# First MoE's first layer on scaled fp16 pairs, its weights converted two chunks at a time

## The chip, the cores and the metric

One core of one Trainium2 chip runs the kernel. The metric is the device time of one execution in microseconds (us), the median of several runs; lower is better. Beside it one execution was recorded by the hardware profiler; all rows of a trace come from such an execution.

## The reference

Causal attention with a cumulative bias over 4 batches of 8 heads, 576 tokens of 64 dimensions, then two pairs of layers (MoE blocks) over the 2304 tokens:

```python
cum = np.cumsum(np.maximum(s, 0.0), axis=-1)
bias = -(cum[:, :, :, None] - cum[:, :, None, :])
scores = np.where(causal, -1e9, q @ k.T / 8 + np.minimum(bias, 0.0))
attn = softmax(scores)                       # rows; then attn @ v
x = heads_to_columns(attn @ v)               # (2304, 512), float32
h = x @ moe_w_in                             # (512, 2048)
x = (h * np.tanh(np.log1p(np.exp(h)))) @ moe_w_out
h = x @ moe2_w_in
out = (h / (1.0 + np.exp(-1.702 * h))) @ moe2_w_out
```

The weights come as float64, everything else as float32.

## The kernel before

Precision is kept by splitting each factor of a product in a high and a low part and summing three products (`mm3`, L814: high x high, high x low, low x high). In attention's scores and in the first MoE both parts are fp32r tiles; in the second MoE both are fp16, after a scaling by a power of two.

**First MoE's first layer.** Tokens are taken in nine units of 256 (`U`), the 2048 hidden columns in 16 chunks of 128 (`NF`). For a unit and a chunk `l1_mm` (L819) issues 4 x 3 matmuls of 128x256. `first_layer` (L968) does units 0 to 6 (192 matmuls each, group "h<-xh,w" in the trace) while attention still runs: after each chunk `slot_a` lets a share of attention's steps (`tick`, L680) pass. The last two units are done together after attention (L1071, group "acc<-xh,w"), then the products with w_out ("acc<-gh,w"). The results go to HBM (`h_d`) by way of "hs" tiles.

**The weights of that layer.** A chunk arrives as 512 KB of float64 words (`fetch_w`, L742; tile "wst"). It is turned to float32 in three instructions (ScalarE Prelu on the high words, VectorE shift of the low words, VectorE join), then split: ScalarE copies the high part, POOL subtracts to get the low part (`turn_w` L764; in the ordered start `turn_words`, `turn_join`, `turn_parts`, L792 to L812). Chunks 0 to 4 are converted in the ordered start, the others by `bg_a` (L835), three chunks ahead of their use. Twelve chunks are fetched at once (`UP`). Raw chunks and converted ones share pool `wa_p` of 16 buffers of 4 KB; "hs" and the maxima's loads "vl" come from `mo_a` (`MA` = 5).

**x.** When a tile of 128 tokens is done, `emit_tile` (L619) transposes it on TensorE ("xt"), ScalarE copies the high part to the unit's tile ("xh"), VectorE subtracts for the low one.

**Order.** From L852 to L937 `nc.mode = "strict"` ties every instruction to the one before it on its engine, so in this start (the first six of attention's steps, chunks 0 to 4, x of unit 0) each engine keeps the order of the code; `warm(n)` there issues n matmuls that compute nothing. Behind it a planner orders the work by its own costs and readiness; what an engine then executes is a fixed in-order list. Attention's steps of batches 1 to 3 send the probabilities through a DMA transpose ("pt<-hl"); their use waits `LAG` steps. PSUM has 8 banks: 4 for attention's tiles ("s", `ps_s`), 3 for "h", 1 for "o".

## Time and profile before

| | us |
|---|---|
| median of 3 runs | 1001.59 (1001.03 to 1003.63) |
| the profiled execution | 1001.29 |
| its span, first to last instruction | 999.3 |
| TensorE busy | 968.8 (97%) |
| VectorE busy | 676.8 (68%) |
| ScalarE busy | 554.3 (55%) |
| POOL busy | 289.1 (29%) |

PE is TensorE's matmuls, PEld its weight loads, which overlap them; DVE is VectorE, ACT ScalarE, POOL GpSimd. Ends of matmuls are modelled, so the mean of one is a latency: for the rate one reads how many of them start in a stretch. The profile attributes almost all instructions to L79, a helper that records them, so groups are told apart by the names of their tiles.

### The profile page before, as it was taken

Reading aid. Unit: us, or ns where it says so; the run is one execution under the profiler, and the core shown is the slowest. Engines: PE = TensorE matmul, PEld = TensorE weight load, DVE = VectorE, ACT = ScalarE, POOL = GpSimd, SP = SyncE. Lnnn points to the kernel's source line nnn. Section 1 sums busy time; section 2 is a strip of 40 time slices with the busy share of each in tenths; the row PEclk is TensorE's granted clock in tenths of the full one; section 3 lists DMA queues with packets and bytes.
Section 4 is the critical chain, followed back from the end, with each engine's and each line's share of the span. In section 5 each row is a group of like instructions: output and inputs, shape, how many; then the busy total and the mean of one; then the engine's idle time right before and its main releaser. Section 6 shows DMA issues by size and latency. Waiting matters only on the chain.

```text
span 999.3 us, 20234 instructions
## 1 busy us (share of the span) xinstructions
PE 968.8 (97%) x7974; PEld 863.0 (86%) x7974; DVE 676.8 (68%) x1363; ACT 554.3 (55%) x1062; POOL 289.1 (29%) x358
## 2 busy tenths in 40 slices
PE   8989998989999999999999999999999999999997
PEld 6868996979889889998888888888888888888886
DVE  6878677774666874788997967985554654653553
ACT  5656577785667874786565845643333433333331
POOL 5636442442144330000000000054342424333341
PEclk9999999999999999999999999999999999999999
DMA  9931688996689977899995653400100100000000
GB/s 257 342 88 40 186 192 166 178 239 149 157 167 223 191 144 188 308 330 357 380 308 181 233 187 107 127 1 16 49 22 1 44 23 1 22 22 1 22 13 32
DMA packets 157262, 142.26 MB, mean 142 GB/s; under 512 B 90000, under 2 KB 126352, under 8 KB 157168
## 3 DMA queue, kind: packets, MB, share of 16 engines
q1 hardware_dynamic: 150240, 122.22, 43.9%
q0 software_dynamic: 6928, 18.75, 6.9%
q8 instruction: 63, 1.03, 0.4%
q14 instruction: 31, 0.25, 0.1%
HBM read 89.09 MB, written 32.58 MB: 122 GB/s over the span
## 4 chain that ended last, share of the span: by engine, by line
PE 83%; DMA 5%; DVE 4%; issue 2%; ACT 1%; POOL 0%; SPq 0%; DVEq 0%; POOLq 0%; ACTq 0%
PE h L79 31%; PE acc L79 25%; PE p L79 16%; PE s L79 5%; PE o L79 3%; DMA pt<-hl 3%; PE kt L79 1%; PE qt L79 1%; DMA qraw<-in_q_dram 1%; PE pt L79 1%; DMA vraw<-in_v_dram 1%; DVE w2l L79 1%; PE xt L79 0%; DVE P L79 0%; DMA vl<-in_v_dram 0%
## 5 line engine op out<-in xcount | busy, mean ns | idle before, releaser
L79 PE MATMUL h<-x,w2i 128*128 128x256 f16 x1728 | 199.8, 273 | 0.9 <-DVE z L79 0.9
L79 PE MATMUL h<-xh,w 128*128 128x256 f32 x1344 | 189.7, 290 | 1.7 <-POOL w L79 0.9
L79 PEld LDWEIGHTS <-w2i 128*128 128x128 f16 x1728 | 169.0, 98 | 20.7 <-issue 1.1
L79 PE MATMUL acc<-gh,w 128*128 128x512 f32 (+1 forms) x640 | 181.7, 369 | 0.0
L79 PEld LDWEIGHTS h<-xh,w 128*128 128x128 f32 x1344 | 169.1, 192 | 4.1 <-ACT w L79 1.5
L79 PE MATMUL p<-w2h,gl 128*128 128x256 f16 x504 | 136.1, 273 | 0.5 <-DVE gl L79 0.5
L79 PE MATMUL p<-w2l,gh 128*128 128x256 f16 x504 | 136.1, 273 | 0.0
L79 PEld LDWEIGHTS acc<-gh,w 128*128 128x128 f32 x640 | 116.1, 189 | 20.6
L79 PE MATMUL p<-w2h,gh 128*128 128x256 f16 x504 | 133.5, 273 | 0.2 <-DVE e L79 0.2
L79 PE MATMUL acc<-gl,w 128*128 128x512 f32 (+1 forms) x320 | 117.9, 368 | 0.0
L79 POOL TENSOR_TENSOR s<-z 128x256 f32<-128x256 f32 x72 | 54.8, 783 | 216.9 <-DVE z L79 213.3
L79 DVE TENSOR_TENSOR gl<-z,gh 128x1024 fp32r<-128x1024 f32 (+1 forms) x72 | 94.4, 1313 | 26.8 <-ACT gh L79 26.1
L79 ACT ACTIVATE sg<-h,spx 128x512 f32<-128x512 f32 x72 | 49.0, 680 | 110.5 <-PE h L79 110.5
L79 PEld LDWEIGHTS <-gh 128*128 128x128 f16 x1008 | 98.6, 98 | 11.7 <-issue 0.3
L79 DVE SCALAR_TENSOR_TENSOR z<-h,sg 128x512 f32<-128x512 f32 x72 | 49.5, 687 | 72.3 <-ACT sg L79 72.3
L79 ACT ACTIVATE P<-P,mx 128x384 f32<-128x384 f32 (+4 forms) x128 | 76.5, 599 | 34.8 <-DVE mx L79 33.1
L79 DVE TENSOR_TENSOR gl<-s,gh 128x1024 f16<-128x1024 f32 x36 | 44.3, 1232 | 64.3 <-ACT gh L79 64.3
L79 DVE CUSTOM_DVE_ANT_0 P<-s,ck 128x384 f32<-128x384 f32 (+4 forms) x128 | 61.6, 497 | 34.2 <-PE s L79 26.8
L79 ACT ACTIVATE gh<-z 128x1024 fp32r<-128x1024 f32 (+1 forms) x72 | 67.9, 947 | 28.5 <-DVE z L79 25.4
L79 ACT ACTIVATE gh<-s 128x1024 f16<-128x1024 f32 x36 | 38.0, 1057 | 81.3 <-POOL s L79 81.3
L79 PE MATMUL s<-kw,qw 128*128 128x288 f32 (+4 forms) x352 | 78.5, 333 | 3.1 <-DVE mx L79 1.8
L79 DVE SCALAR_TENSOR_TENSOR wst<-wst 128x512 int32<-128x512 int32 x96 | 70.9, 755 | 2.8 <-ACT wst L79 2.5
(146 smaller groups left out, 1635.1 us busy)
## 6 DMA issues: line engine op xcount, KB each, us to landing
h_d<-hs SPq DMA_DIRECT2D x36, 512.0 KB, 4.6
hg<-h_d SPq DMA_DIRECT2D x36, 512.0 KB, 6.2
wst<-in_moe_w_in_dram SPq DMA_DIRECT2D x32, 512.0 KB, 7.2
wst<-in_moe_w_out_dram SPq DMA_DIRECT2D x32, 512.0 KB, 6.1
x_d<-x SPq DMA_DIRECT2D x18, 256.0 KB, 3.4
out_dram<-o SPq DMA_DIRECT2D x9, 512.0 KB, 2.8
kraw<-in_k_dram POOLq DMA_DIRECT2D x32, 128.0 KB, 4.7
w_d<-w2y SPq DMA_DIRECT2D x16, 256.0 KB, 5.1
```

Source lines behind the costliest of these rows:

```text
L79: r = f(*a, **kw)
```

## The change

The first layer of the first MoE goes from fp32r parts to fp16 parts of scaled numbers. The weights are scaled per pair of chunks by a power of two, from a sum of absolute values: ScalarE sums each row (Abs with an accumulator), a bf16 matrix of ones on TensorE sums over the rows (`over_rows`), VectorE makes the scale. x of batches 1 to 3 keeps the scale that v had (now a power of two, no longer divided out in `norm_tile`), x of batch 0 is scaled per unit by v's maxima (`v_peak`, `x_scale`). The eviction from PSUM multiplies by the inverse scales (`evict`), in two pieces where a unit crosses a batch. Chunks are converted in pairs, by two queues of stages (`pair_a`, `pair_b`, `pairs_to`); the low part of a pair's first chunk is made by VectorE, that of its second by POOL in two instructions. A pair of chunks takes one 4 KB buffer instead of two; "hs" and "vl" tiles move to that pool. Sizes and lags change (`MA`, `MBB`, `HLB`, `PTB`, `LAG`).

```diff
-MA = 5
-MBB = 2
+MA = 2
+MBB = 5
-HLB = 3
+HLB = 4
-PTB = 5
-WAH = 3
-NP0 = 5
-FROM = 7
+PTB = 7
-LAG = 4
+LAG = 5
...
+    def to_scale(t, src, tiny, top):
+        nc.vector.tensor_scalar(out=t, in0=src, scalar1=tiny, scalar2=1.0 / top, op0=ALU.max, op1=ALU.mult)
+        nc.vector.reciprocal(t, t)
+        pow2(t)
+
+    def over_rows(cols, n):
+        ps = ps_s.tile([128, 512], F32, tag="s", name="bd")
+        nc.tensor.matmul(out=ps[:, 0:n], lhsT=ones, rhs=cols, start=True, stop=True, skip_group_check=True)
+        return ps[:, 0:n]
...
+    def v_peak(i, g):
+        n = min(128, S - 128 * i)
+        peak(vm0[:n, 2 * i + g:2 * i + g + 1], vt[0, i, g][:n].rearrange("p h d -> p (h d)"))
+
+    def x_scale(k, ni):
+        t = sm_p.tile([128, 2], F32, tag="sx", name="sx", bufs=3)
+        ps = over_rows(vm0[:, 0:2 * ni], 2 * ni)
+        nc.vector.tensor_reduce(out=t[:, 0:1], in_=ps, axis=mybir.AxisListType.X, op=ALU.max)
+        to_scale(t[:, 0:1], t[:, 0:1], 1.0e-30, VTOP)
+        ev_table(k, t)
...
-            t = tmp_pair(F32, "vl")[:, 0:VW]
+            t = wa_p.tile([128, 1024], F32, tag="w", name="vl")[:, 0:VW]
...
-                xunit[u] = xh_a.tile([128, 2, KC, U], F32R, tag="xh", name="xh")
+                xunit[u] = xh_a.tile([128, 2, KC, U], F16, tag="xh", name="xh")
...
+            if b:
+                nc.scalar.activation(out=hi, in_=src, func=AF.Copy)
+                nc.vector.tensor_tensor(out=lo, in0=src, in1=hi, op=ALU.subtract)
+            else:
+                k_ = f"u{u}"
+                k_ = sx[k_][:, 0:1]
+                nc.scalar.activation(out=hi, in_=src, func=AF.Copy, scale=k_)
+                nc.vector.scalar_tensor_tensor(out=lo, in0=src, scalar=k_, in1=hi, op0=ALU.mult, op1=ALU.subtract)
...
+    def pair_sum(p):
+        wsm[p] = ws = sm_p.tile([128, 2], F32, tag="wsm", name="wsm")
+        for e in range(2):
...
+            lut(junk, y, AF.Abs, accum_out=ws[:, e:e + 1])
+
+    def pair_a(p):
+        pair_words(p)
+        pair_join(p)
+        pair_sum(p)
+
+    def pair_col(p):
+        wmx[p] = t = sm_p.tile([128, 2], BF16, tag="wmx", name="wmx")
+        nc.vector.tensor_copy(t, wsm.pop(p))
+
+    def pair_scale(p):
+        ps = over_rows(wmx.pop(p), 2)
+        wkp[p] = k = sm_p.tile([128, 2], F32, tag="wk", name="wk")
+        k = k[:, 0:1]
+        nc.vector.tensor_reduce(out=k, in_=ps, axis=mybir.AxisListType.X, op=ALU.max)
+        to_scale(k, k, TINY, WTOP1)
+        nc.vector.reciprocal(isw[:, p:p + 1], k)
+
+    def pair_parts(p):
+        k = wkp.pop(p)[:, 0:1]
+        win_t[p] = t = wa_p.tile([128, 2, 2, DM], F16, tag="w", name="w")
+        for e in range(2):
+            y = fetched.pop((0, 2 * p + e, "in"))
+            hi, lo = t[:, e, 0, :], t[:, e, 1, :]
+            nc.scalar.activation(out=hi, in_=y, func=AF.Copy, scale=k)
+            if e:
+                nc.gpsimd.tensor_scalar(out=y, in0=y, scalar1=k, scalar2=None, op0=ALU.mult)
+                nc.gpsimd.tensor_tensor(out=lo, in0=y, in1=hi, op=ALU.subtract)
+            else:
+                nc.vector.scalar_tensor_tensor(out=lo, in0=y, scalar=k, in1=hi, op0=ALU.mult, op1=ALU.subtract)
+        fetch_a()
...
+    def pairs_to(pa, pb):
+        for k, f, n in ((0, pair_a, pa), (1, pair_b, pb)):
+            while wq[k] < min(n, NF // 2):
...
```

The ordered start: the steps of the chunks leave it, those of pairs 0 and 1 come in:

```diff
     early_pt(steps[0])
     warm(12)
-    turn_words(0)
+    pair_words(0)
+    for g in range(2):
+        v_peak(0, g)
     score(2)
     early_turn(1, 1)
+    early_pt(steps[1])
+    pair_join(0)
+    early_av(steps[0])
+    score(3)
     load_group(0, 2, 0, False)
...
-    early_pt(steps[1])
-    turn_join(0)
-    early_av(steps[0])
-    turn_parts(0)
-    turn_words(1)
-    score(3)
     early_pt(steps[2])
     early_av(steps[1])
-    turn_join(1)
-    turn_parts(1)
-    emit_tile(steps[1])
-    turn_words(2)
+    pair_sum(0)
+    for g in range(2):
+        v_peak(1, g)
+    emit_tile_turn(steps[1])
+    x_scale("u0", 2)
+    emit_tile_parts(steps[1])
     score(4)
+    pair_col(0)
     early_pt(steps[3])
     early_av(steps[2])
-    turn_join(2)
+    pair_scale(0)
+    pair_words(1)
     score(5)
-    turn_parts(2)
-    turn_words(3)
+    pair_parts(0)
+    pair_join(1)
     early_pt(steps[4])
     early_av(steps[3])
     warm(10)
-    turn_join(3)
+    pair_sum(1)
     early_pt(steps[5])
-    turn_parts(3)
-    turn_words(4)
     warm(4)
+    pair_col(1)
     early_av(steps[4])
+    pair_scale(1)
     early_av(steps[5])
-    turn_join(4)
-    emit_tile(steps[5])
-    turn_parts(4)
+    emit_tile_turn(steps[5])
     warm(8)
+    emit_tile_parts(steps[5])
+    pair_parts(1)
...
     def first_layer(u, xr, each):
         for m in range(0, NF, 4):
-            t = tmp_pair(F32, "hs")
+            t = wa_p.tile([128, 1024], F32, tag="w", name="hs")
...
-                    while wq and (0, min(NF - 1, m + 2 * e + d + WAH)) not in win_t:
-                        bg_a()
+                    p = (m + 2 * e) // 2
+                    pairs_to(p + 4 + d, p + 2 + d)
...
-                nc.scalar.activation(out=o, in_=ps, func=AF.Copy)
+                evict(o, ps, m // 2 + e, u * U, (u + 1) * U, 2)
```

## Rows read from the trace of the kernel before

**Rows 1.** Stages: length, busy PE, PEld, DVE, ACT, POOL (instructions), clock, DMA share, GB/s.

```profile
15.00:36.00 21.00, 17.89 (x133) 15.40 (x131) 16.13 (x34) 11.57 (x30) 5.23 (x4) 0.92 1.10 342
36.00:105.00 69.00, 63.08 (x497) 55.95 (x497) 56.40 (x122) 44.57 (x103) 41.81 (x48) 1.00 0.41 125
105.00:392.00 287.00, 274.84 (x2669) 250.84 (x2667) 200.51 (x553) 205.93 (x523) 97.32 (x131) 0.99 0.84 179
392.00:439.00 47.00, 47.00 (x391) 46.71 (x389) 32.98 (x55) 33.56 (x53) 0.61 (x1) 1.00 0.90 310
439.00:637.00 198.00, 198.00 (x965) 167.18 (x963) 167.61 (x321) 121.28 (x161) 2.31 (x3) 1.00 0.72 250
```

**Rows 2.** TensorE's groups by shape: count | busy us, mean ns | idle before.

```profile
L79 PE MATMUL h<-x,w2i 128*128 128x256 f16 x1728 | 199.8, 273 | 0.9 <-DVE z L79 0.9
L79 PE MATMUL h<-xh,w 128*128 128x256 f32 x1344 | 189.7, 290 | 1.7 <-POOL w L79 0.9 <-ACT w L79 0.8
...
L79 PE MATMUL acc<-xh,w 128*128 128x256 f32 x384 | 46.9, 284 | 0.0
...
L79 PEld LDWEIGHTS h<-xh,w 128*128 128x128 f32 x1344 | 169.1, 192 | 4.1 <-ACT w L79 1.5 <-POOL w L79 1.1 <-DVE xh L79 0.2
L79 PEld LDWEIGHTS <-w2i 128*128 128x128 f16 x1728 | 169.0, 98 | 20.7 <-issue 1.1
```

**Rows 3.** The chain that ended last: start us, us, what.

```profile
225.66 11.94 PE h L79 x93
...
701.93 2.62 PE h L79 x24
```

**Rows 4.** TensorE in order of time: start us, us, instruction, count.

```profile
35.83 8.29 PE L79 MATMUL h<-xh,w 128*128 128x256 f32 x64
...
103.13 1.36 PE L79 MATMUL h<-xh,w 128*128 128x256 f32 x10
...
396.06 42.84 PE L79 MATMUL acc<-xh,w 128*128 128x256 f32 x352
438.73 0.40 PE L79 MATMUL acc<-gh,w 128*128 128x512 f32 x1
```

**Rows 5.** VectorE in order of time, 15 to 60 us, idle time before in brackets.

```profile
15.91 0.43 DVE L79 TENSOR_SCALAR wst<-wst 128x512 int32<-128x512 int32 x1 [2.30 <-DMA wst<-in_moe_w_in_dram]
17.78 0.68 DVE L79 SCALAR_TENSOR_TENSOR wst<-wst 128x512 int32<-128x512 int32 x1
...
30.46 1.33 DVE L79 SCALAR_TENSOR_TENSOR wst<-wst 128x512 int32<-128x512 int32 x1 [0.53 <-ACT wst L79]
...
35.81 0.69 DVE L79 TENSOR_TENSOR xh<-xt,xh 128x512 fp32r<-128x512 f32 x1 [0.56 <-ACT xh L79]
...
59.77 0.69 DVE L79 TENSOR_TENSOR kw<-kt,kw 64x512 fp32r<-64x512 f32 x1 [4.95 <-ACT kw L79]
```

**Rows 6.** VectorE's groups by shape, 0 to 105 us.

```profile
L79 DVE SCALAR_TENSOR_TENSOR wst<-wst 128x512 int32<-128x512 int32 x16 | 17.2, 1101 | 0.5 <-ACT wst L79 0.5
...
L79 DVE COPY k<-qk 128x256 f32<-128x256 f32 x4 | 1.7, 418 | 0.4 <-PE qk L79 0.3
```

**Rows 7.** VectorE in order of time: first and last of five small ones.

```profile
546.49 0.16 DVE L79 TENSOR_REDUCE rk<-wim 128x1 f32<-128x4 f32 x1
...
547.26 0.16 DVE L79 RECIPROCAL rk<-rk 128x1 f32<-128x1 f32 x1
```

**Rows 8.** ScalarE's groups by shape, 0 to 105 us.

```profile
L79 ACT ACTIVATE P<-P,mx 128x512 f32<-128x512 f32 x8 | 5.8, 721 | 4.7 <-DVE mx L79 4.6
```

**Rows 9.** POOL's groups by shape, 0 to 392 us.

```profile
L79 POOL TENSOR_TENSOR w<-wst,w 128x512 fp32r<-128x512 f32 x16 | 21.6, 1360 | 24.3 <-ACT w L79 23.8 <-POOL ck L79 0.3
L79 POOL COPY ck<-ck 64x512 f32<-64x512 f32 x24 | 17.1, 713 | 35.5 <-DVE mx L79 29.1 <-DVE rs L79 5.7
```

**Rows 10.** TensorE's waits, 105 to 392 us: total us, times, longest.

```profile
PE o L79 <- DMA pt<-hl: 7.1, 6, 2.7
```

**Rows 11.** Busy time of each engine, 290 to 337 us; columns as in rows 1.

```profile
290.00:337.00 47.00, 46.72 (x468) 43.45 (x467) 35.10 (x111) 37.48 (x100) 19.83 (x28) 1.00 1.04 210
```

More of the change, by code (lines that the diff above doesn't have):

```diff
@@ L307, in split_items, with ev_table, ev_need, x_class @@
         return [qT], [v1, v2] if b else [], kT
+    vm0 = sm_p.tile([128, 2 * NTIL], BF16, tag="vm0", name="vm0", bufs=1)
+    def v_peak(i, g):
[7 more added lines that the diff above has]
+        ev_table(k, t)
+    def ev_table(k, t):
+        sx[k] = t
+        nc.vector.reciprocal(t[:, 1:2], t[:, 0:1])
+    def ev_need(k):
+        if k not in evs:
+            evs[k] = e = const.tile([128, NF // 2], F32, name=f"ev{k}")
+            if k != "u0":
+                nc.vector.tensor_scalar(out=e, in0=isw, scalar1=sx[k][:, 1:2], scalar2=None, op0=ALU.mult)
+        return evs[k]
+    def x_class(t0, t1):
+        r = []
+        while t0 < t1:
+            b = t0 // S
+            m = min(t1, (b + 1) * S)
+            r.append((t0, m, b if b else f"u{t0 // U}"))
+            t0 = m
+        return r
     vsc, vmx = {}, {}
@@ L762, in fetch_w, with to_f32 @@
         fetched[lay, m, kind] = r
-    def turn_w(pool, lay, m, kind):
-        t = pool.tile([128, 2, DM], F32R, tag="w", name="w")
-        (win_t if kind == "in" else wout_t)[lay, m] = t
-        r = fetched.pop((lay, m, kind))
-        th, tl_ = t[:, 0, :], t[:, 1, :]
-        if not wide:
-            nc.scalar.activation(out=th, in_=r, func=AF.Copy)
-            nc.vector.tensor_tensor(out=tl_, in0=r, in1=th, op=ALU.subtract)
-            return
+    def to_f32(r, first):
         zi, yi = r[:, :, 0], r[:, :, 1]
         y = yi.bitcast(F32)
-        sided = lay == 0 and kind == "in"
-        if sided:
+        if first:
             held(lut(y, y, AF.Prelu, scale=2.0 ** -112, alpha=-(2.0 ** 32)))
@@ L781, in turn_w @@
         nc.vector.scalar_tensor_tensor(
-            out=yi if sided else zi, in0=yi, scalar=3, in1=zi, op0=ALU.logical_shift_left, op1=ALU.bitwise_or
+            out=yi if first else zi, in0=yi, scalar=3, in1=zi, op0=ALU.logical_shift_left, op1=ALU.bitwise_or
         )
-        if not sided:
+        if not first:
             nc.vector.scalar_tensor_tensor(
@@ L814, in mm3, with pair_b, turn_w @@
+    def pair_b(p):
+        pair_scale(p)
+        pair_parts(p)
+    def turn_w(pool, lay, m, kind):
+        t = pool.tile([128, 2, DM], F32R, tag="w", name="w")
+        wout_t[lay, m] = t
+        r = fetched.pop((lay, m, kind))
+        th, tl_ = t[:, 0, :], t[:, 1, :]
+        y = to_f32(r, False) if wide else r
+        nc.scalar.activation(out=th, in_=y, func=AF.Copy)
+        nc.vector.tensor_tensor(out=tl_, in0=y, in1=th, op=ALU.subtract)
     def mm3(outp, hi_w, lo_w, hi_x, lo_x, start, stop):
@@ L827, in attention_moe_moe_kernel @@
     nxt = [0]
-    wq = list(range(NP0, NF))
+    wq = [0, 0]
     fq = list(range(NF))
@@ L867, in attention_moe_moe_kernel @@
     nc.gpsimd.memset(cumb[96:128], 0.0)
+    nc.gpsimd.memset(ones, 1.0)
+    nc.gpsimd.memset(vm0, 0.0)
     nc.vector.tensor_copy(identb, ident)
@@ L874, in attention_moe_moe_kernel @@
         v_load(i_, g, nc.sync)
-    for _ in range(UP):
+    while len(fq) > NF - UP:
         fetch_a()
@@ L1077, in attention_moe_moe_kernel @@
             l1_mm(ps[:, d * U:(d + 1) * U], 0, m, xl[d], d == 0)
-        nc.scalar.activation(out=o, in_=ps, func=AF.Copy)
+        evict(o, ps, m // 2, (NU - UE) * U, NT, 1)
         if m % 2:
```

112 lines of the change are left out of this document (71 added, 41 removed).

## The prediction

> **What bounds the kernel now.** I read the windows by stage first. From 105 to 392 us, where attention and units 1 to 6 of the first MoE's first layer run together, TensorE is busy 274.84 of 287 us, VectorE 200.51 and ScalarE 205.93; from 392 to 439 us (the last two units) and from 439 to 637 us TensorE has no gap at all [rows 1]. Before that it is different: from 15 to 36 us TensorE is busy 17.89 of 21 us, partly with warm-up matmuls that compute nothing, and VectorE works 16.13; from 36 to 105 us TensorE is at 63.08 and VectorE at 56.40 of 69 us. So there are two regimes: a start paced by chains through VectorE and ScalarE, and a long part paced by TensorE. The change makes the second cheaper and the first dearer, and the sum is the difference of the two.
>
> Then the groups by shape. The first layer's matmuls are 1344 + 384 of 128x256 in two-part fp32r, 290 and 284 ns each; the second MoE's same shape in fp16 pairs takes 273 ns [rows 2]. These are latencies and overlap; what counts is the distance between two. The chain has 93 fp32r matmuls in a row in 11.94 us, 128.4 ns each, and 24 in fp16 in 2.62 us, 109.2 ns each [rows 3]. The last two units run 352 from 396.06 to 438.73 us: 121.2 ns each [rows 4]. The weight loads say why: 192 ns for an fp32r load against 98 in fp16, and in the first layer the loads alone fill 169.1 us for 1344, 125.8 ns each [rows 2]. In fp32r the weight load is the pitch; in fp16 it falls below the 109 ns of the matmul.
>
> **Part 1: the matmuls.** Same count, same three products, operands now fp16. For units 0 to 6 I take the load's 125.8 ns as the old pitch, for the last two units their own 121.2, and 109.2 as the new one. Units 1 to 6: 6 x 192 x 16.6 ns = 19.1 us. The last two units: 384 x 12.0 ns = 4.6 us. Unit 0's 192 would be 3.2 us, but I count them at nothing: VectorE paces that stretch (part 3). Bounds by the other pitches: 1152 x 12.0 = 13.8 to 1152 x 19.2 = 22.1 us for units 1 to 6.
> The 4.6 us are kept only if what follows is ready earlier too. The next thing, the w_out products, starts at 438.73 us [rows 4]; beside it VectorE has 167.6 of 198 us of work [rows 1] and TensorE has no gap there, so I keep all of it; the bound from below is 0.
>
> **Part 2: the ordered start, up to unit 0's first matmul.** In this stretch each engine keeps the order of the code. Unit 0's first matmul runs at 35.83 us [rows 4], just as its last x part is made at 35.81 [rows 5]. I follow VectorE's queue from 15.91 us, where it waited 2.30 us for the first chunk of weights [rows 5]. The pair needs two chunks before the next score may pass: the second chunk's transfer follows at some 1.5 us (512 KB at the 342 GB/s of that stretch [rows 1]). Then, ahead of unit 0, VectorE loses the work of one chunk (one shift and one join, about 1.0 us at the uncontended 0.68 us a join) and gains: four v maxima of 128x256 at some 0.35 (a copy of that size takes 418 ns, its successor starts earlier [rows 6]) = 1.4; one x scale and two pair scales of five small instructions each, as those from 546.49 to 547.42 us, 0.93 us a chain [rows 7] = 2.8; two column copies, 0.3; one low part (pair 0's) at 0.6. Sum 1.5 + 1.4 + 2.8 + 0.3 + 0.6 - 1.0 = 5.6 us. ScalarE gains four Abs passes with their accumulator reads (an exponential of 128x512 takes 721 ns [rows 8]; I count 0.7 with the read) and loses one chunk; it is less full, but pair 0's low part now waits for ScalarE behind score 5, about 1 us more. The waits that are added: VectorE's first instruction of each scale waits for the ones product on TensorE, and behind it stand the next shifts and the next score's minimum, for which ScalarE's exponentials and TensorE's transposes wait in turn; the ones product itself stands in TensorE's queue ahead of scores. I take **+6.6 us** on unit 0's first matmul. From below: the 4.9 us that VectorE idles in 15 to 36 us [rows 1] could swallow most of it, +2; from above, +9, with every hop between engines paid.
>
> **Part 3: the rest of unit 0.** Six pairs remain. Each adds on VectorE a scale chain 0.93, a column copy 0.15 and a low part that POOL made until now, 0.6: 1.7 us, 10.2 in all. Six more v maxima 2.1, two x scales 1.9, the eviction factors of unit 0 about 1.2. Sum 15.4 us of new VectorE work from 36 to 105 us, where it idles 12.6 [rows 1]. One hole is 4.95 us, waiting at 59.77 for a k turn [rows 5]; work that comes late fills that one wholly, and I count half of the other 7.6: 8.8 us absorbed, **+6.6**. With all idle used it is +2.8, with none +15.4.
> POOL works less in this stretch: 16 subtractions of 1360 ns become 8, with 8 multiplications by a scalar that the trace doesn't have, between a copy's 713 and the 1360 [rows 9]; I take 0.9, nearer the copy, as both have one input: 21.8 to 18 us. That matters for VectorE: a join beside a POOL subtraction took 1.33 us, and the 16 joins average 1101 ns [rows 5, 6] against 0.68 alone. 4 us less of POOL give back about **-1.0**.
> The Trainium skill (GPSIMD Engine Reference, Key points) speaks against the step here: POOL shares its SBUF interfaces with VectorE, to the cost of VectorE instructions with two SBUF inputs. The joins at 1101 ns agree with it. The low parts moved to VectorE have two SBUF inputs as well; stretched like the joins, 8 x 0.42 us, they would take 3.4 us more, and the sum below would end 3.4 us higher.
> Start and unit 0 together: 6.6 + 6.6 - 1.0 = **+12.2 us**, from +4 to +22.
>
> **Part 4: edits that I cost near nothing.** The h tiles and v maxima's loads move to the pool of the weights, whose 16 buffers now hold 8 pairs instead of 16 chunks; the freed memory deepens the transposes' buffers (5 to 7, 3 to 4) and the lag before a tile is used grows from 4 steps to 5. Cover for more lag is the step's other work; its gain is at most the 7.1 us that TensorE waits for transposes after 105 us [rows 10], its loss a step longer tail. I take -2, bounds -5 and +3. Evictions get a scale (free on ScalarE) and split in three units at a batch boundary: 24 extra instructions of some 0.3 us on ScalarE, 7 us beside its 205.93 of 287 [rows 1]. The loads of tile 2 move behind score 3 in the code, but POOL, which issues them, is busy 5.23 of those 21 us [rows 1] and has nothing ahead of them; SP fetches the last four chunks as pairs 0 to 3 are split, ahead of no transfer that this stretch needs. Both cost nothing; without that cover, an issue more or less, under 1 us. The evictions are hidden if ScalarE has room: (206 + 7)/266 = 0.80, and in 290 to 337 us it already runs at 37.48 of 47 while TensorE is busy 46.72 [rows 11].
>
> **The sum.** The profiled execution took 1001.29 us (span 999.3 and 2.0 outside it), the median of the runs is 1001.59. -19.1 - 4.6 + 12.2 - 2.0 = -13.5: **988 us**, 1.3% less.
>
> **Rivals.** *The start is nearly free.* VectorE's idle time in both stretches (4.9 + 12.6) takes in the new work, the start costs +4: -21.7, 980 us. For it: the sum of idle time. Against: one engine's queue is in order there and each hole has its own reason.
> *Nothing is absorbed.* Start +22: -3.7, 998 us. For it: each pair is a chain ScalarE, VectorE, TensorE, VectorE, ScalarE, and every hop stalls what is queued behind it.
> *Part of the matmul gain is lost to attention.* In units 1 to 6 half of the 19.1 us returns as waits for exponentials and transposes: -4.0, 997 us.
> *Slower.* Attention's chain, not TensorE, paces units 1 to 6: a step takes as long as before, since ScalarE and the transposes' transfers (DMA busy share 0.84 [rows 1]) can't run denser than now. Then the 19.1 us are lost and no lag helps: +12.2 - 4.6 = +7.6, 1009 us. It decides as soon as more than 11.5 of the 19.1 are lost (12.2 - 4.6 - 19.1 = -11.5 without the lag's 2). For it: all the waits after 105 us are for DMA or VectorE. Against: they are only some 12 of 287 us, and 290 to 337 us shows both engines denser [rows 11].
> *It doesn't do what it says*: fp16 in this layer runs at the old pitch. The fp16 rows of the same shape exclude nearly all of it; then only the costs are left, 12.2 - 2.0 = +10.2, 1012 us.
>
> **How the numbers follow.** Chances: forecast (981 to 995 us) 0.56; start nearly free 0.14; part lost to attention 0.11; nothing absorbed 0.08; slower 0.09; not as it says 0.02. The range 977 to 1003 us leaves out the last two and a bit of the second; its lower end is the free start with the lag's best case, its upper the unabsorbed start with the lag's worst. A measurement of this kernel tells some 0.3% from no change, 998.6 to 1004.6 us: faster 0.56 + 0.14 + 0.08 of the attention case + 0.01 of the unabsorbed start = 0.79; within 0.3%: 0.03 + 0.07 = 0.10; slower 0.11.
>
> **What would show it.** A pitch of 109 ns in a long run of first-layer matmuls and weight loads of 98 ns: part 1. Unit 0's first matmul at 41 to 44 us instead of 35.83, VectorE without the 4.95 us hole and unit 0's last matmul some 8 to 14 us later than now, where its last group starts at 103.13 [rows 4]: parts 2 and 3. From there to the w_out products some 24 us less than now, with ScalarE near 0.8. Wrong would be: unit 0 starting before 39 us, a last group of unit 0 at or before 103 us, or TensorE idle over 25 us between unit 1 and the last two units.

## The result and the profile after

The changed kernel takes 1009.96 us (median of 11 runs, 1005.68 to 1012.14), the kernel before 1001.9 in the same comparison (11 runs): ratio 1.0068, 95% interval 1.0048 to 1.0089. It is slower by 0.7% where 1.3% faster was forecast. Its profiled execution took 1012.14 us, span 1010.1. (Times of one kernel differ by 4 to 17 us between runs; so below, totals are medians with the interval of their ratio to the kernel before, and places are read from one trace each. The two traces lie 10.8 us apart, the medians 8.1.)

The same stages as [rows 1], of the changed kernel:

```profile
15.00:36.00 21.00, 15.88 (x104) 12.82 (x103) 14.55 (x40) 11.18 (x31) 1.27 (x1) 0.84 1.10 345
36.00:105.00 69.00, 53.82 (x384) 43.08 (x385) 58.83 (x159) 47.90 (x114) 36.64 (x38) 0.90 0.34 104
105.00:392.00 287.00, 267.20 (x2681) 228.85 (x2680) 211.64 (x596) 214.53 (x555) 108.93 (x145) 0.98 0.86 180
392.00:439.00 47.00, 44.52 (x445) 38.59 (x442) 28.59 (x55) 29.61 (x50) 1.65 (x2) 0.96 0.82 261
439.00:637.00 198.00, 198.00 (x969) 165.93 (x967) 167.37 (x318) 127.56 (x170) 1.55 (x2) 1.00 0.72 260
```

From 36 to 105 us TensorE falls from 63.08 us busy to 53.82, and the granted clock from 1.00 to 0.90; VectorE and ScalarE are only a little fuller than before. TensorE in order of time, which answers to [rows 4]:

```profile
42.74 3.44 PE L77 MATMUL h<-xh,w 128*128 128x256 f16 x30
...
60.85 2.07 PE L77 MATMUL kt<-ident,kraw 128*128 128x128 f32 x8 [4.54 <-ACT kraw L77]
...
91.73 2.46 PE L77 MATMUL h<-xh,w 128*128 128x256 f16 x12
...
96.89 1.27 PE L77 MATMUL h<-xh,w 128*128 128x256 f16 x10
...
125.84 1.27 PE L77 MATMUL h<-xh,w 128*128 128x256 f16 x10
...
400.55 0.49 PE L77 MATMUL acc<-xh,w 128*128 128x256 f16 x3
403.05 0.60 PE L77 MATMUL o<-v,pt 128*64 128x128 f16 x18 [2.01 <-DMA pt<-hl]
403.58 5.44 PE L77 MATMUL acc<-xh,w 128*128 128x256 f16 x33
408.86 0.38 PE L77 MATMUL xt<-ident,x 128*128 128x128 f32 x2
409.71 38.15 PE L77 MATMUL acc<-xh,w 128*128 128x256 f16 x348 [0.47 <-ACT xh L77]
447.62 0.47 PE L77 MATMUL acc<-gh,w 128*128 128x512 f32 x1
```

Unit 0's first matmul moves from 35.83 to 42.74 us (+6.9), its last group from 103.13 to 125.84 (+22.7), the start of the last two units from 391.99 to 400.55 (+8.6), that of the w_out products from 438.73 to 447.62 (+8.9). The end comes 10.8 us later. So up to unit 0's last group 22.7 us are lost, units 1 to 6 bring back 14.1, the last two units nothing.

Unit 0's last group is not a pure mark of delay, though. From unit 0's first matmul to its last group, the kernel before and then the changed one (length, busy PE, PEld, DVE, ACT, POOL, clock, DMA share, GB/s):

```profile
35.83:103.13 67.30, 61.38 (x482) 54.32 (x481) 55.79 (x120) 44.27 (x102) 40.28 (x46) 1.00 0.41 125
```

```profile
42.74:125.84 83.10, 69.20 (x542) 56.96 (x539) 72.12 (x204) 56.82 (x135) 47.63 (x52) 0.94 0.29 84
```

TensorE's idle time in it grows from 5.9 to 13.9 us; the other 7.8 us are busy time. Part of that runs at a lower clock, and 542 matmuls start there instead of 482: more of attention's steps stand ahead of the last group, and from there to the last two units 66 fewer are left to do. Part of the 22.7, and of the 14.1 that come back, is work in another place. TensorE's idle time is the safer measure: up to unit 0's first matmul it grows by 3.6 us, in unit 0 by 8.0, in units 1 to 6 by 7.3 (12.2 to 19.5).

The pitch itself is as forecast: 38.15 us for 348 matmuls are 109.6 ns each, and a weight load takes 99 ns (groups by shape, as [rows 2]):

```profile
L77 PE MATMUL h<-xh,w 128*128 128x256 f16 x1344 | 169.4, 275 | 3.1 <-ACT w L77 1.6 <-DVE w L77 1.4
...
L77 PEld LDWEIGHTS <-w 128*128 128x128 f16 x1728 | 165.2, 99 | 25.3 <-ACT w L77 2.1 <-DVE w L77 1.8 <-issue 0.6
```

Now the same columns up to the start of the last two units, the kernel before and then the changed one:

```profile
0.00:391.99 391.99, 368.85 (x3381) 331.99 (x3381) 280.78 (x725) 268.51 (x677) 154.35 (x208) 0.99 0.78 179
```

```profile
0.00:400.55 400.55, 358.49 (x3375) 302.16 (x3375) 297.43 (x822) 285.74 (x731) 158.15 (x210) 0.96 0.78 177
```

TensorE's idle time grew from 23.1 to 42.1 us (+18.9), its busy time fell by 10.4 only; together they are the 8.6 us by which the last two units start later. By the new pitch the busy time should fall by 1344 x 16.6 ns = 22.3 us, so 11.9 are missing. Most of that is the clock: in its stretches at 1.2 GHz TensorE is busy for 24.0 us here and for 6.8 in the kernel before, and half of each, 12.0 - 3.4 = 8.6 us, is an estimate of what they cost. The pitch itself gave some 20 us: a kernel below, e11, does the same matmuls in 346.70 us, 22.2 less than before, of which the same estimate gives 1.9 to the clock.

**The clock.** In the kernel before, TensorE is granted 1.2 instead of 2.4 GHz for 6.8 us in all before the end of the work; in the changed one for 37.5 us, at 22, 39, 60, 90, 227, 404 and 660 us. Four windows of the changed kernel, columns as above, two of these falls each with the stretch ahead of it:

```profile
18.00:22.10 4.10, 1.12 (x8) 0.55 (x6) 3.96 (x11) 2.13 (x7) 0.00 (x0) 1.00 1.09 336
22.10:28.90 6.80, 6.29 (x26) 4.79 (x27) 5.01 (x16) 3.00 (x9) 0.00 (x0) 0.50 1.10 349
53.00:59.60 6.60, 2.18 (x16) 1.48 (x15) 6.01 (x11) 3.71 (x8) 4.52 (x5) 1.00 0.85 243
59.60:66.40 6.80, 5.55 (x25) 4.69 (x26) 4.21 (x11) 4.42 (x14) 1.52 (x2) 0.50 0.45 150
```

TensorE was busy 1.12 of 4.10 and 2.18 of 6.60 us ahead of them, waiting for others; then its own work took longer: 12 first-layer matmuls 2.46 us at 91.73 (205 ns each) against 10 in 1.27 at 96.89 (127 ns).

These are two executions, and the clock differs between executions of one kernel too. Each has its mean granted clock on record: 0.987 to 0.998, in the mean 0.993, in 96 executions of the kernel before beside the experiments; 0.976 to 0.983, in the mean 0.979, in the 11 of the changed one. As time at 1.2 GHz that is some 14 us (4 to 26) against 42 (34 to 48). By a line through the 96, 1 us more at 1.2 GHz goes with 0.42 us more time. By that estimate the 27 us more cost some 11 us, which is more than the whole loss of 8.1.

**Waits.** TensorE's waits from 105 to 392 us for the transposes, against 7.1 us before [rows 10]: the waits did not get shorter with the longer lag and the deeper buffers.

```profile
PE o L77 <- DMA pt<-hl: 12.8, 10, 4.7
```

**POOL.** Its groups up to 128 us, then some rows in order of time, against [rows 9]:

```profile
L77 POOL TENSOR_SCALAR wst<-wst,wk 128x512 f32<-128x512 f32 x8 | 15.7, 1960 | 45.3 <-ACT w L77 24.4 <-DVE w L77 20.8
...
L77 POOL TENSOR_TENSOR w<-wst,w 128x512 f16<-128x512 f32 x8 | 9.7, 1212 | 0.5
```

```profile
43.52 2.39 POOL L77 TENSOR_SCALAR wst<-wst,wk 128x512 f32<-128x512 f32 x1 [4.96 <-ACT w L77]
45.99 1.51 POOL L77 TENSOR_TENSOR w<-wst,w 128x512 f16<-128x512 f32 x1
47.42 0.81 POOL L77 DMA_DIRECT2D qraw<-in_q_dram  x1
48.23 3.45 POOL L77 DMA_DIRECT2D v<-in_v_dram  x5
51.67 2.24 POOL L77 DMA_DIRECT2D kraw<-in_k_dram  x3
```

The multiplication by the pair's scale takes 1960 ns, more than the subtraction with two inputs. The Trainium skill (GPSIMD Engine Reference, 4.1 Engine selection) calls GpSimd about twice as slow on two inputs and roughly at line rate on one; the subtraction, 1212 ns against 687 for the same one on VectorE in e11, agrees with the first half, the multiplication does not with the second, and the measurement decides. The loads of the next tiles stand in POOL's queue behind pair 1's part, and those of kraw go out from 51.67 us on. But they land 2.6 to 2.8 us after their issue, and the 4.54 us that TensorE waits for the k turns at 60.85 are not theirs. ScalarE's step for that turn stands behind a pass over absolute values, which waited for a join on VectorE:

```profile
59.14 0.66 ACT L77 ACTIVATE wst<-wst 128x512 f32<-128x512 f32 x1 [2.88 <-DVE wst L77]
...
60.40 0.40 ACT L77 ACTIVATE kraw<-kraw 128x256 f32<-128x256 f32 x1
```

And ahead of that join VectorE has four v maxima and two shifts that took 1.92 us together, beside POOL's subtraction at 56.35, where two took 0.74 at 30.81. So work that the change brought holds up attention's, through in-order queues.

**A scale's chain.** The longest of the eight, VectorE in order of time (the rows between, attention's and other conversions' work, left out), then its ones product on TensorE and the split that uses the scale on ScalarE:

```profile
79.30 0.15 DVE L77 TENSOR_REDUCE wk<-bd 128x1 f32<-128x2 f32 x1
79.37 0.54 DVE L77 CUSTOM_DVE_ANT_0 P<-s,ck 128x384 f32<-128x384 f32 x1
...
80.84 0.14 DVE L77 TENSOR_SCALAR wk<-wk 128x1 f32<-128x1 f32 x1
...
82.93 0.15 DVE L77 RECIPROCAL wk<-wk 128x1 f32<-128x1 f32 x1
...
84.92 0.15 DVE L77 TENSOR_SCALAR wk<-wk 128x1 int32<-128x1 int32 x1
```

```profile
75.84 0.17 PE L77 MATMUL bd<-wmx,ones 128*128 128x2 bf16 x1
```

```profile
86.15 1.41 ACT L77 ACTIVATE w<-wst,wk 128x512 f16<-128x512 f32 x2
```

Four instructions of 0.15 us took 10.3 us from end to end, because each stands behind others in a full queue. The other seven chains took 2.4 to 6.7 us (3.4 in the ordered start).

### The profile page after: what moved, and what is told of

Its sections match the earlier page's. It is cut to its first block, busy times and chain, and to the rows that moved or that the text cites. A ratio compares the mean times of both kernels' runs of the same rounds, so it can differ in the third digit from the quotient of the medians.

```text
span 1010.1 us, 20396 instructions
## 1 busy us (share of the span) xinstructions
PE 957.9 (95%) x7985; PEld 826.3 (82%) x7985; DVE 692.7 (69%) x1460; ACT 572.4 (57%) x1118; POOL 293.7 (29%) x360
## 4 chain that ended last, share of the span: by engine, by line
PE 78%; DMA 9%; DVE 6%; ACT 3%; issue 2%; SPq 1%; POOL 0%; DVEq 0%; ACTq 0%; POOLq 0%
PE h L77 27%; PE acc L77 24%; PE p L77 16%; DMA pt<-hl 5%; PE s L77 4%; PE o L77 3%; DMA kraw<-in_k_dram 2%; PE kt L77 1%; PE qt L77 1%; DVE wst L77 1%; DMA wst<-in_moe_w_in_dram 1%; DVE p L77 1%; ACT P L77 1%; PE pt L77 1%; PE xt L77 1%
## 5 line engine op out<-in xcount | busy, mean ns | idle before, releaser
L77 PEld LDWEIGHTS <-w 128*128 128x128 f16 x1728 | 165.2, 99 | 25.3 <-ACT w L77 2.1
L77 PE MATMUL h<-xh,w 128*128 128x256 f16 x1344 | 169.4, 275 | 3.1 <-ACT w L77 1.6
L77 PE MATMUL s<-kw,qw 128*128 128x288 f32 (+4 forms) x352 | 83.8, 350 | 1.1 <-DVE p L77 0.6
L77 DVE CUSTOM_DVE_ANT_0 P<-s,ck 128x384 f32<-128x384 f32 (+4 forms) x128 | 61.6, 497 | 30.1 <-PE s L77 22.4
L77 POOL DMA_DIRECT2D x<-x_d x5 | 3.8, 766 | 235.7 <-DMA wst<-in_moe_w_in_dram 179.0
```

The source lines that it names most:

```text
L77: r = f(*a, **kw)
```

## The experiments

Theories of why the change costs what it costs: (A) the conversion's new work on VectorE, above all the chains that measure peaks; (B) GpSimd's share of a pair; (C) TensorE's clock, falling as TensorE waits; (D) the longer lag; (E) the fp16 matmuls give less than the sum said, since attention paces units 1 to 6. All kernels were timed against the kernel before. In the table: ratio with its interval; the start of unit 0's last group, of the last two units, and of the w_out products; TensorE's idle time up to the last two units; time at 1.2 GHz before the end of the work (all us, from one trace); and the mean granted clock of all executions of the kernel.

| kernel | ratio | unit 0 | last two | w_out | idle | 1.2 GHz | clock, all |
|---|---|---|---|---|---|---|---|
| before | 1 | 103 | 392 | 439 | 23.1 | 7 | 0.993 |
| changed | 1.0068 [1.0048, 1.0089] | 126 | 401 | 448 | 42.1 | 38 | 0.979 |
| e1 weights' scale fixed | 0.9934 [0.9900, 0.9968] | 99 | 389 | 434 | 35.5 | 31 | 0.982 |
| e2 all scales fixed | 0.9986 [0.9955, 1.0016] | 95 | 392 | 439 | 38.9 | 34 | 0.981 |
| e3 multiplication on ScalarE | 0.9921 [0.9890, 0.9952] | 111 | 390 | 437 | 31.6 | 34 | 0.984 |
| e7 low parts on VectorE | 0.9950 [0.9933, 0.9967] | 112 | 391 | 438 | 33.1 | 31 | 0.985 |
| e14 = e1 + e7 | 0.9895 [0.9851, 0.9938] | 86 | 385 | 430 | 30.1 | 27 | 0.985 |
| e13 = e2 + e7 | 0.9876 [0.9828, 0.9925] | 85 | 384 | 428 | 31.6 | 31 | 0.988 |
| e16 = e13, LAG 4 | 0.9946 [0.9911, 0.9980] | 85 | 387 | 436 | 33.5 | 27 | 0.985 |
| e4 LAG 4, old buffers | 1.0029 [1.0010, 1.0049] | 126 | 392 | 440 | 36.6 | 24 | 0.981 |
| e9 LAG 4 | 1.0005 [0.9979, 1.0031] | 125 | 391 | 439 | 34.6 | 31 | 0.981 |
| e6 more warm-up | 0.9982 [0.9955, 1.0008] | 121 | 395 | 439 | 32.7 | 31 | 0.986 |
| e10 = e3 + e4 + e6 | 1.0013 [0.9986, 1.0040] | 114 | 395 | 441 | 28.9 | 38 | 0.982 |
| e5 before on fp16 | 0.9820 [0.9779, 0.9862] | 106 | 384 | 428 | 29.9 | 17 | 0.989 |
| e12 before, LAG 5 | 0.9953 [0.9933, 0.9973] | 103 | 390 | 437 | 19.4 | 17 | 0.994 |
| e8 = e5 + LAG 5 | 0.9801 [0.9762, 0.9840] | 107 | 376 | 419 | 26.6 | 10 | 0.991 |
| e15 before, low parts on VectorE | 0.9951 [0.9922, 0.9980] | 94 | 384 | 431 | 17.0 | 3 | 0.992 |
| e17 = e15 + LAG 5 | 0.9893 [0.9839, 0.9947] | 98 | 387 | 435 | 15.2 | 17 | 0.994 |
| e11 = e8 + low parts on VectorE | 0.9734 [0.9675, 0.9793] | 92 | 367 | 410 | 20.4 | 3 | 0.993 |

**The arithmetic alone: e5.** The kernel before with fp16 parts and constant scales that suit these inputs (256 for the weights, 4096 for x); no peak is measured.

```diff
-            nc.scalar.activation(out=hi, in_=src, func=AF.Copy)
+            nc.scalar.activation(out=hi, in_=src, func=AF.Copy, scale=XK)
...
-        t = pool.tile([128, 2, DM], F32R, tag="w", name="w")
+        t = pool.tile([128, 2, DM], F16 if kind == "in" else F32R, tag="w", name="w")
...
-        nc.scalar.activation(out=o, in_=ps, func=AF.Copy)
+        nc.scalar.activation(out=o, in_=ps, func=AF.Copy, scale=2.0 ** -20)
```

> The kernel before, with its own order, pools and lags, and only the parts of the first layer in fp16: weights times the constant 256 (in the first ScalarE pass, no instruction more), x times 4096, the eviction times 2^-20; no scale is measured. It is part 1 of the prediction by itself. If TensorE paces units 1 to 6: -19.1 - 4.6 and up to 3.2 for unit 0, 975 to 979 us. If attention's chain takes part of it: 980 to 995 us. If attention's chain takes all of it: 998 us or more.

988.79 us, 0.982: a gain of 18 us (14 to 22), not the 23.7 of the sum, nor the 26.9 with unit 0's 3.2. TensorE's idle time grew by 6.8 us, its waits for pt<-hl from 7.1 to 12.5. So part of the gain turns into waits even where nothing else is changed, and most of these waits are attention's. And the loss of the changed kernel, 0.7%, is 2.5% against this one: what came with the arithmetic costs some 25 us, not the forecast 10.

**Measuring the peaks: e1, e2.** e1 takes constant 8 for the weights' scale and leaves their measuring out; e2 also x's of batch 0.

```diff
-            lut(junk, y, AF.Abs, accum_out=ws[:, e:e + 1])
...
-        ps = over_rows(wmx.pop(p), 2)
...
-        k = wkp.pop(p)[:, 0:1]
+        k = 8.0
```

> The changed kernel without the measurement of the weights' scale: no Abs pass, no column, no ones product, no five small instructions per pair; the scale is the constant 8, the power of two that the measurement gives for these weights. Theory A (the measurement's chain and its VectorE work make the start long): VectorE loses 8 x 1.1 = 9 us and the chain a hop through TensorE, unit 0's last group from 125.84 to 112 to 117 us, the time 1010.0 - 9 to 14: 996 to 1001 us. Theory B (POOL's multiplication by a scalar, 1960 ns and two POOL instructions in a row, makes the start long): 1006 to 1010 us. Theory C (the clock falls because TensorE idles in the start, and the fall makes the rest): some of it comes back with the shorter idles, 1000 to 1005 us.

> As before, and x of batch 0 has the constant scale 32768 (what the measurement gives here) in place of ten maxima and three chains on VectorE. Theory A: another 10 x 0.4 + 3 x 0.9 = 7 us less VectorE work, of which half counts: 992 to 998 us, unit 0's first matmul at 38 to 40 us instead of 42.74. Theory B: 1004 to 1009 us. Theory C: 998 to 1003 us, with the clock at 0.99 or more.

e1: 998.35 us, 0.993, within theory A's 996 to 1001; unit 0's last group at 98.5 instead of 125.8, earlier than its 112 to 117. The measuring of the weights costs the kernel 13 us. Of the 27 us at unit 0 only 5.4 are idle time of TensorE (13.9 to 8.5); the rest is mostly that 369 matmuls start in that stretch instead of 542:

```profile
43.57:98.52 54.95, 46.43 (x369) 39.43 (x368) 48.95 (x109) 37.26 (x83) 33.65 (x34) 0.89 0.30 94
```

e1 leaves out the chains on VectorE and also ScalarE's 16 passes over absolute values (some 0.85 us each with the read of the accumulator, 13.6 us in all); no run keeps one and drops the other. e2: unit 0 is ready 4 us earlier still, but the time is 1004.26, not better than e1, and theory A's 992 to 998 is missed. To bring unit 0 forward is not enough: the steps of attention that no longer stand in it come in units 1 to 6.

**GpSimd: e3, e7.** e3 moves POOL's multiplication to ScalarE, e7 both of its instructions to VectorE.

```diff
-            nc.scalar.activation(out=hi, in_=y, func=AF.Copy, scale=k)
             if e:
-                nc.gpsimd.tensor_scalar(out=y, in0=y, scalar1=k, scalar2=None, op0=ALU.mult)
+                nc.scalar.activation(out=y, in_=y, func=AF.Copy, scale=k)
+            nc.scalar.activation(out=hi, in_=y, func=AF.Copy, scale=1.0 if e else k)
+            if e:
```

```diff
-            if e:
-                nc.gpsimd.tensor_scalar(out=y, in0=y, scalar1=k, scalar2=None, op0=ALU.mult)
-                nc.gpsimd.tensor_tensor(out=lo, in0=y, in1=hi, op=ALU.subtract)
-            else:
+            if True:
                 nc.vector.scalar_tensor_tensor(out=lo, in0=y, scalar=k, in1=hi, op0=ALU.mult, op1=ALU.subtract)
```

> The changed kernel with POOL's multiplication moved to ScalarE (its own scaled copy, some 0.6 us); POOL only subtracts, as in the kernel before. Theory A: within 2 us of the changed kernel, 1008 to 1012. Theory B: each pair's second half is ready 1.4 us earlier, VectorE loses the stalls beside 15.7 us of POOL work, the loads behind it in POOL's queue leave earlier: unit 0's last group at 115 to 119 us, 1000 to 1004 us. Theory C: between, with more clock where TensorE idles less.

> The changed kernel with both low parts of a pair on VectorE (8 more operations of 0.75 us there by its own undisturbed rows, 6 us), GpSimd doing none of the conversion (25.4 us less there). Theory VectorE: VectorE has no gap from 67 to 95 us and paces unit 0; its 6 us more lengthen the time by 3 to 6 us, 1013 to 1016. Theory GpSimd: the pair's GpSimd operations (1960 and 1212 ns) stretch VectorE's operations beside them and hold up the pairs and the loads queued behind them; without them unit 0 ends by 105 to 113 us, as with the multiplication moved to ScalarE (111.0), and the time is 996 to 1002.

998.45 and 998.05 us, 0.992 and 0.995, unit 0 at 111.0 and 112.2: about 14 us earlier in both, and 12 to 15 us off the time, more than theory B gave e3 and as theory GpSimd had e7. TensorE's idle time in unit 0 falls by some 5 us in both, the rest of the 14 is mostly that 448 and 460 matmuls start there instead of 542. That VectorE's load by itself paces unit 0 is refuted by e7, which gives VectorE eight instructions more. All sixteen last 766 ns each there, without POOL's part of the conversion beside them, against 934 for the eight in the changed kernel (VectorE's groups up to 128 us, e7):

```profile
L77 DVE SCALAR_TENSOR_TENSOR w<-wst,wk,w 128x512 f16<-128x512 f32 x16 | 11.8, 766 | 1.8 <-ACT w L77 1.8
```

**Both: e14, e13.** e14 is e1 and e7 together, e13 e2 and e7.

> The changed kernel without measuring the weights' peaks (constant 8), x still measured, both low parts of a pair on VectorE. Each alone gave 0.993 and 0.995. If the two delays lie one behind the other in a pair's conversion, their gains add: 0.981 to 0.986. If both only bring unit 0's end forward, and attention's steps take that back in units 1 to 6: 0.989 to 0.995.

> The changed kernel without any measuring of peaks (fixed scales for weights and for batch 0's x) and with both low parts of a pair on VectorE: of the change, the ordered start in pairs, the staged conversion of six chunks and the longer lag stay. Fixed scales alone gave 0.999, low parts on VectorE alone 0.995; the kernel before on fp16 parts, lag 5, low parts on VectorE gave 0.973. If GpSimd's share and the measuring are all that stands between the changed kernel and that one: 0.970 to 0.980 and half-clock stretches under 10 us. If the ordered start itself keeps TensorE idle and its clock low: half-clock stretches of 20 to 35 us and 0.985 to 0.995.

0.9895 and 0.9876. The two delays do not add up: the changed kernel's ratio falls by 0.013 for e1, 0.012 for e7 and 0.017 for both. Unit 0 is then ready at 85 us, earlier than in any kernel of the old order, but the last two units start at 384. And e13 stays 1.4% behind e11, which has the same arithmetic, the same lag and no part of the conversion on POOL, but the old order of the start, conversion by single chunks, the old buffers and evictions by a constant. TensorE up to the last two units, e13 and then e11:

```profile
0.00:384.17 384.17, 352.53 (x3364) 301.07 (x3364) 283.02 (x757) 273.52 (x699) 132.88 (x200) 0.96 0.83 184
```

```profile
0.00:367.05 367.05, 346.70 (x3363) 294.96 (x3364) 282.93 (x741) 263.97 (x676) 134.02 (x192) 1.00 0.84 191
```

11.3 us more of idle time, and 5.8 us more for the same matmuls at a clock of 0.96 instead of 1.00.

**The lag: e4, e9, e12, e16.** e4 sets LAG, PTB and HLB back in the changed kernel; e9 LAG alone; e12 puts LAG 5 into the kernel before; e16 is e13 with e4's edit.

```diff
-LAG = 5
+LAG = 4
...
-HLB = 4
+HLB = 3
-PTB = 7
+PTB = 5
```

> The changed kernel with LAG 4, PTB 5 and HLB 3 as before, its ordered start and its fp16 pairs kept. The prediction gave the longer lag and the buffers a gain of 2 us (from 5 gained to 3 lost), so by it this run is some 2 us longer than the changed kernel: about 1012, TensorE's waits for pt<-hl above 14.8 us. Rival: the lag brings nothing or costs, because the waits for pt<-hl doubled from 7.1 us (before) to 14.8 us with it: then 1003 to 1008, and those waits fall back towards 7 us. Unit 0's end stays at 120 to 128 us either way.

> The changed kernel with LAG 4 alone, its larger buffers (PTB 7, HLB 4) kept. With LAG 4 and the smaller buffers the ratio to the kernel before was 1.003 against 1.007 for the changed kernel, and TensorE waited 7.8 us instead of 14.8 for pt<-hl. If the longer lag makes these waits: again 7 to 9 us of them and 1.001 to 1.004. If the buffers made them: 12 to 15 us and 1.005 to 1.008.

> The kernel before, nothing changed but LAG 5 instead of 4 (first layer still on fp32r parts). The prediction's part 4 gave the lag and the buffers a gain of 2 us (5 gained to 3 lost): 0.995 to 1.003 and fewer waits for pt<-hl than the 7.1 us before. Rival, that a longer lag lengthens the waits as in the changed kernel: waits of 9 to 15 us and 1.002 to 1.006.

> The changed kernel without any measuring of peaks, both low parts on VectorE (measured: 0.988, TensorE waiting 14.4 us for pt<-hl), and now LAG 4, PTB 5, HLB 3 as before. No peak is measured. If the longer lag, by its waits for the transposes, is what still stands between 0.988 and the 0.973 of the kernel before on fp16 parts: waits of 5 to 9 us and 0.974 to 0.982. If it is the ordered start and attention's order behind it: 0.984 to 0.992 whatever the waits.

The signs differ. In the changed kernel lag 4 is faster (1.003 and 1.0005 against 1.007), with unit 0 untouched at 125 and 126 us and the waits for pt<-hl over the whole execution at 7.8 and 8.5 us instead of 14.8; the buffers change nothing that e4 and e9 can tell apart. In the kernel before lag 5 is faster by 0.5%, waits 2.5 instead of 7.1. In e13 lag 4 with the old buffers is slower by 0.7%, which the two intervals do not quite separate, waits 13.5 instead of 14.4. The waits, of the changed kernel with lag 4 (e4) and of the kernel before with lag 5 (e12):

```profile
PE o L77 <- DMA pt<-hl: 7.8, 8, 2.2
```

```profile
PE o L79 <- DMA pt<-hl: 2.5, 1, 2.5
```

So no price of the lag by itself comes out of these runs. As I read them it depends on the order in which the planner then puts the rest, and a change of it is a new draw worth 0.4 to 0.7% one way or the other.

**The clock: e6.** 52 more warm-up matmuls in the start.

```diff
     early_turn(1, 1)
+    warm(18)
     early_pt(steps[1])
     pair_join(0)
+    warm(10)
     early_av(steps[0])
...
-    warm(4)
+    warm(28)
```

> The changed kernel with 52 more warm-up matmuls (128x256 bf16) in the ordered start, at three places where TensorE waits. Theory of the clock: the granted clock falls to half because TensorE idles in the start, and the half-clock stretches (37 us in the changed kernel against 6.8 before) make a good part of the late end of unit 0: then the stretches at 22, 39 and 60 us go, unit 0 ends 4 to 8 us earlier and the time is 1002 to 1006. Theory of the engines: VectorE and GpSimd pace the start and unit 0, TensorE waits for them at either clock: unit 0's end moves by under 2 us and the time stays at 1008 to 1012.

1000.6 us, 0.998: 0.9% less, more than either theory gave; unit 0's last group comes 4.8 us earlier, as the theory of the clock had it. In the trace the fall at 22 us is gone, the others moved (13.7 us of 1.2 GHz from 52.6), and the total is 31 us. Over all executions the time at 1.2 GHz fell from some 42 us to 28 (14 to 38, 10 runs); at the 0.42 us for each that the kernel before shows, that is an estimated 5 to 6 of the 8.6 us. So theory C is likely to have a share in the loss, but the rest of the order changed as well: of 10.8 us between the two spans 3.8 lie in the last two units (from 47.1 to 43.3 us), where the wait for a transpose and the fall at 404 us are missing.

**Three together: e10.** e3's multiplication, e4's lag and buffers, e6's warm-up.

> The changed kernel with three edits together: the multiplication on ScalarE instead of GpSimd (alone 0.992), LAG 4 with PTB 5 and HLB 3 (alone 1.003), 52 more warm-up matmuls in the start (alone 0.998), the changed kernel itself 1.007. If the three act at different places (unit 0's pairs, the transposes of units 1 to 6, the clock in the start and in the last two units): 0.980 to 0.986. If each only removes the same stall, or attention's chain takes back what unit 0 gains: 0.989 to 0.994.

1006.09 us, 1.001, worse than e3 alone and outside both ranges; 37.5 us at 1.2 GHz. Single gains of 0.4 to 1.5% don't add. With every edit the planner orders the work after the start anew, and the falls of the clock land elsewhere.

**The best order, and the arithmetic in it: e8, e11, e15, e17.** e8 is e5 with LAG 5. e11 is e8 with the weights' low parts on VectorE (the edit below, and the same in `turn_w`). e15 is the kernel before with that edit, e17 also with LAG 5, both still fp32r; e8 and e11 keep e5's constant scales.

```diff
-        nc.gpsimd.tensor_tensor(out=t[:, 1, :], in0=y, in1=t[:, 0, :], op=ALU.subtract)
+        nc.vector.tensor_tensor(out=t[:, 1, :], in0=y, in1=t[:, 0, :], op=ALU.subtract)
```

> The kernel before with its first layer on fp16 parts at fixed scales (measured: 0.982 of the time before, waits for pt<-hl 12.5 us in all), and LAG 5 instead of 4, buffers unchanged (PTB 5, HLB 3). The fixed scales leave out the measuring of the peaks. If the transposes' waits come from the shorter ticks of the fp16 units and a longer lag covers them, as the prediction's part 4 had it: waits for pt<-hl under 9 us and 2 to 6 us faster than without the longer lag, 0.976 to 0.980. If the lag does not help (the buffers or the DMA queue bound the transposes): waits of 11 to 16 us and 0.981 to 0.988.

> The kernel before on fp16 parts at fixed scales with LAG 5 (measured: 0.980), the low parts of its weights on VectorE instead of GpSimd (16 x 1.19 us less there, 16 x 0.75 us more on VectorE). Fixed scales leave out the measuring of the peaks. If GpSimd's part of the conversion as such holds up unit 0, also in the order of the kernel before: unit 0's last matmuls at 95 to 102 us instead of 106.9 and 0.974 to 0.979. If GpSimd's part was only too long in the changed kernel because of its slow multiplication (1960 ns), and VectorE is the fuller engine here: unit 0 ends at 106 to 112 us, 0.980 to 0.988.

> The kernel before with nothing changed but the low parts of the first layer's weights on VectorE instead of GpSimd (16 x 1.36 us less there, 16 x 0.75 us more on VectorE), still fp32r. With fp16 parts and lag 5 this edit brought unit 0's end from 106.9 to 92.3 us and 0.980 to 0.973. If GpSimd's part costs that also without fp16: unit 0 ends at 90 to 97 us and 0.990 to 0.996. If the gain needed the fp16 parts: 0.998 to 1.004.

> The kernel before with the low parts on VectorE (alone 0.995) and LAG 5 (alone 0.995), first layer still on fp32r parts: against the kernel with the same order on fp16 parts (0.973, 977.7 us) it prices the arithmetic by itself. The prediction's part 1 gave 1152 x 16.6 ns + 384 x 12.0 ns = 23.7 us, and 192 x 16.6 ns = 3.2 us more in unit 0 where TensorE paces it: 0.997 to 1.000, if all of it comes through. If attention paces units 1 to 6 and takes part of it back, the two stand 10 to 18 us apart: 0.984 to 0.992.

e8 is at 0.980, with 4.9 us of waits for pt<-hl instead of e5's 12.5; e11 is at 0.973 (977.69 us), the fastest of all. POOL's part costs the kernel before 0.5% too (e15: unit 0 at 93.7 instead of 103.1). fp16 against fp32r in the same order: 0.9820 against 1, 0.9801 against 0.9953, 0.9734 against 0.9893, so 18, 15 and 16 us, each uncertain by 4 to 8; the first two exclude 23.7. In the last pair TensorE's row for fp32r (e17), to be held against e11's above:

```profile
0.00:387.11 387.11, 371.93 (x3364) 334.96 (x3364) 284.71 (x741) 266.70 (x676) 133.90 (x192) 0.98 0.82 181
```

Busy falls by 25.2 us. Half of the time that TensorE works at 1.2 GHz is 8.1 us in e17 and 1.5 in e11, so by this estimate 6.6 of it are the clock and 18.6 the pitch, less than the 22.3 of the sum; idle time grows by 5.2. The last two units take 43.3 us instead of 47.5, a gain of 4.2. That is theory E: the pitch itself is worth some 4 us less than the sum said, and about 5 more turn into waits.

## Why the prediction was wrong

The forecast was -13.5 us, and the two traces lie +10.8 apart. Of the 24.3 us between them 0.3 lie ahead of unit 0 (part 2), 10.2 in unit 0 (part 3), 7.0 in units 1 to 6 (part 1 and the lag), 4.9 in the last two units and 1.9 behind them.

**Part 1** was right in the new pitch (109.6 ns for 109.2, loads 99 ns for 98) and too high in what arrives: 23.7 us in the sum, 15 to 18 us by three pairs of kernels in the same order. The rival "part of the matmul gain is lost to attention" was true: in units 1 to 6 TensorE's idle time grew by 7.3 us, 5.7 of them in the waits for pt<-hl. Of the last two units' 4.6 us nothing arrived in the changed kernel, 4.2 in e11: 348 matmuls ran at the new pitch, but ahead of them stand 2.01 us of waiting for a transpose and 33 matmuls in 5.44 us, 165 ns each, part of them at the lower clock. The bound of nothing there was right, its reason (what follows must be ready) was not: the gap opened in front.

**Part 2** was right in its sum: +6.9 for +6.6, and VectorE waits for the two chunks at 16.30 and 17.77, 1.47 us apart for the 1.5 forecast. The split is partly luck. From the first chunk to the last x part VectorE's work grew by 2.5 us where the terms say 4.1, its waiting by 3.4 where they say 2.5. Warm-up matmuls run up to unit 0's first matmul in both kernels, so neither trace names what released it.

**Part 3** is the step that failed, in its cost and in the path that it took for it: +15.8 us instead of 6.6 - 1.0, just above its own upper end of 15.4. (The +22 given for start and unit 0 together is less than these ends add up to, 9 + 15.4 - 1.0 = 23.4.) It asked how much of VectorE's idle time the new work would fill. From 36 to 105 us VectorE works only 2.4 us more than before, and TensorE waits all the same: 8.0 of the 15.8 us are TensorE's idle time. Some 4.5 are the clock (half of its busy time in the stretches at 60 and 90 us), the new pitch takes 3.2 off, and what is left, some 6.5, is attention's work that now stands there.

Two terms were mis-sized. The multiplication on POOL was taken at 0.9 us and took 1.96, above the bound of 1.36 from the nearest rows: POOL had 25.4 us for the conversion instead of 18, and without the multiplication, or without all of it, the kernel is 12 to 15 us faster (e3, e7). And the scale's chain was priced by the time that it occupies VectorE, 0.93 us; what counts for a pair is the time until it is through a queue in which attention's steps stand between its links, 2.4 to 10.3 us; without the measuring the kernel is 13 us faster (e1). These gains do not add (e14), and e1 takes ScalarE's passes away together with the chains, so how the loss divides between chains, passes, POOL and the order that the planner makes of them stays open. The stretching of the low parts beside POOL, which the prediction put at 3.4 us if they fared like the joins, was 934 against 766 ns, 8 x 0.17 = 1.3 us; the joins, beside less POOL subtraction, fell from 1101 to 766 ns, 5.4 us for 16 where 1.0 was forecast.

**Part 4**: the evictions are hidden, as forecast: among TensorE's waits from 105 to 392 us none is for one. But their scale is not free: 675 against 590 ns for 128x512, and ScalarE has 8.6 us more from 105 to 392 us. The lag's gain of 2 us was wrong in sign here (e4, e9: 4 to 6 us lost) and right in sign in the old order (e12: 4.7 gained). The loads in POOL's queue were costed at nothing for want of work ahead of them; pair 1's part stands ahead of them now, but the k turn that TensorE waited 4.5 us for did not wait for its load.

**Missing from the sum** was the clock: every wait in the start was priced once, at its length. In these two traces 37.5 us at 1.2 GHz instead of 6.8 cost, as estimated above, 8.6 us up to the last two units and some 3 more in the falls at 404 and 660 us. Over all executions it is 42 us instead of 14, at an estimated 11 us.

Of the rivals, "nothing is absorbed" had the start right (+22, measured 22.7) and was 12 us off in the time (998), since it kept the rest of the gains; "slower" had the end right (1009) but by another mechanism: the gain of units 1 to 6 was not lost as a whole (14 us came between the two marks, a part of them work moved into unit 0), the start was dearer. That it hit the number is luck.

**Open** is why e13 stays 1.4% behind e11: ordered start, conversion in pairs, sizes of buffers, evictions and order of the steps all differ. Its clock (0.988 against 0.993) is an estimated 4 of these 14 us. And e10 and the lag's runs show that the order alone can move the time by about as much as a single edit. That TensorE had waited ahead of a fall of the clock is what the windows show for two falls; that fewer waits bring the clock back is what e6 suggests, not shown apart from the changed order.
